# Attention and FFN on one core: another order of weight words, low parts, tanh product and attention in the first sixteen FFN steps

## The chip, the cores and the metric

The kernel runs on one core of a Trainium2 chip. The metric is the device time of the whole program in microseconds, over several runs. PE is TensorE (matrix products), PEld its weight loads, DVE is VectorE, ACT is ScalarE, POOL is GpSimd and SP is the engine whose queue issues the transfers.

## The reference

```python
# attention: batch 8, heads 8, sequence 576, head_dim 64
scores = scale * np.matmul(q, k.transpose(0, 1, 3, 2))
mask_local = (rel >= 0) & (rel < 32)                          # heads 0 to 3
mask_strided = (rel >= 0) & (pos[None, :] % 32 == pos[:, None] % 32)   # heads 4 to 7
scores = np.where(masks, scores, -1e9); scores -= max
attn = exp(scores) / (sum(exp(scores)) + 1e-9)
x = (attn @ v) as (4608 tokens, 512)
# FFN: w_in 512 x 2048, w_out 2048 x 512
h = x @ w_in
g = h * (1 / (1 + exp(-1.702 * h)))
out = g @ w_out
```

All inputs and the output are float32.

## The kernel before

Matrix products of the FFN are made from high and low parts. A float32 operand is cast to fp32r (the high part) and the remainder is the low part; one product of two operands is three matmuls (high·high, high·low, low·high). In the tile names `gh`, `gl` are the parts of g, `xhl`, `xll` those of the local half of x, `xhs`, `xls` those of its strided half, and `w` holds both parts of a weight tile.

**FFN.** The 4608 tokens are 9 groups of 512, and the 2048 hidden columns 16 tiles of 128, so there are 144 steps (group, tile). In step s PE computes h of that step (`ffn1`, 12 matmuls of 512 columns) and, two steps late (`LAG`), the product of g with w_out, summed in four PSUM banks `o` over the 16 steps of a group (`ffn2`, 12 matmuls). `act` makes g from h: tanh on ACT, then `(tanh + 1) * h` on DVE into the tile `g`, then gh on ACT and gl on DVE. There are two buffers of gh and gl and one of `g`. Eight PSUM banks: two for scores (`s`), six for h, the value products `a` and the four `o`; a bank of h is free when DVE has read it for g.

**Weight words.** The weights come in a 64-bit form, two 32-bit halves for each element, and are put together on the core once, in group 0. There are 32 words (`items`), two for each step: word 2f-2 is tile f of w_in, word 2f-1 is tile f-2 of w_out, for f from 2 on. A word takes a load into `raw` (SP), a shift of one half (`shift`) and a scaling with sign of the other (`sign`, both on ACT, but every fourth shift on DVE), the join of both (`join`, DVE: the row `raw<-raw` by SCALAR_TENSOR_TENSOR), the cast to the high part (`high`, ACT: `w<-raw`) and the subtraction that gives the low part (`low`, DVE: `w<-raw,w`). `raw` tiles and `w` tiles come out of one pool of 32 slots, so a later tile takes the slot of an earlier one when the last reader of that is done. The load of word k+8 is issued behind `low(k)`. The last word has a tile of its own, `words`.

**Attention.** 42 pairs, strided (three for each batch) and local. A pair's stages are: scores on PE; masked scores and maxima on DVE (two SCALAR_TENSOR_TENSOR into `pr`, then TENSOR_REDUCE); eight exponentials on ACT with their sums; sum and reciprocal on DVE (`rinv`); scaling of `pr` on POOL; transpositions on DVE into `pt` (6 for a strided pair, 8 for a local one, 32x256 each); value products on PE into a bank `a`; and the two parts of x on ACT and DVE. Pairs 0 to 4 are done ahead of step 2 in a prologue, in which the transposing is done by PE (`turn_pr`, bank `t`) and scores go into the banks `s` and `u`. Pairs 5 to 10 (strided, local, strided, local, strided, strided) are spread over the steps of group 0, later ones over the following groups: `TURNS` names the step of the transpositions for each, scores stand two steps behind the transpositions of the pair before the last one, the value products two steps behind a pair's own transpositions.

**What sets the order.** Each engine runs its instructions in the order in which the program writes them; `InOrder` (line 116, and 118 in the changed kernel) records every instruction, so that all rows have that one line and the tile names tell them apart. The main loop starts at step 2. A step of before writes: h of step s; then `act(s - 1, weigh)`, that is tanh and product of the step before with one `weigh` (high, shift and sign of the next, low, join of the next) between product and gh; a second `weigh`; transpositions, values; then scores, maxima and exponentials; then `ffn2(s - 2)`.

Of the kernel before, what the change touches and what calls it, by code (L numbers as in the profile page):

```python
# [9 lines left out]
F32 = mybir.dt.float32  # L10
# [8 lines left out]
P = 128  # L19
# [6 lines left out]
KB = QB + STRIDE  # L26
# [14 lines left out]
G = 512  # L41
NG = B * S // G
NF = DFF // P
# [12 lines left out]
AHEAD = 2  # L56
# [1 line left out]
RAWB = 8  # L58
N0 = 5
ZEROS = {0: 4, 1: 4}  # L60
TURNS = ((4, 7, 9, 12, 13), (0, 3, 6, 9, 12), (2, 8))


def _pairs():
# [17 lines left out]
def attn_ffn(ctx, tc, lqk, sqk, lv, sv, w_in, w_out, masks, out):  # L82
# [7 lines left out]
    ffn = ctx.enter_context(tc.tile_pool(name="ffn", bufs=2))  # L90
    psum = ctx.enter_context(tc.tile_pool(name="psum", bufs=8, space=bass.MemoryType.PSUM))

    def bank(name):
        tag, n = ("s", 2) if name[0] == "s" else ("x", 6)
        return psum.tile([P, 512], F32, tag=tag, name=name, bufs=n)

    def st2(shape, dtype, name):
        return st.tile(shape, dtype, tag="st2", name=name, bufs=NT)
# [5 lines left out]
    n0 = N0  # L104

    class InOrder:
# [15 lines left out]
    vector, scalar, gpsimd, sync, tensor = (  # L122
        InOrder(e) for e in (nc.vector, nc.scalar, nc.gpsimd, nc.sync, nc.tensor)
    )
    matmul, transposed = tensor.matmul, tensor.transpose
# [3 lines left out]
    def w_tile(shape, dtype, name):  # L129
        return wp.tile(shape, dtype, tag="w", name=name, bufs=2 * NF)  # L130
# [32 lines left out]
    zeros = const.tile([P, P], BF16, name="zeros")  # L163
# [3 lines left out]
    first = [[bank(f"{x}{j}") for j in range(2)] for x in "sut"]  # L167
# [8 lines left out]
    def geom(p):  # L176

        kind, a, _ = pairs[p]
        if kind == "s":
            m = masks_sb[:, :NB]  # L180
            return NB, m.unsqueeze(1).broadcast_to([P, 2 * U, NB])
        begins = [i for i in range(2 * U) if (2 * U * a + i) % (S // QB) == 0]
        if not begins:
            m = masks_sb[:, MASK_L + KB : MASK_L + 2 * KB]
            return KB, m.unsqueeze(1).broadcast_to([P, 2 * U, KB])
        at = MASK_L + (0, 2, 3, 1)[begins[0]] * KB
        m = masks_sb[:, at : at + U * KB]
        return KB, m.unsqueeze(1).broadcast_to([P, 2, U * KB])
# [107 lines left out]
    def turn_pr(p):  # L296

        nk, _ = geom(p)
        for i in range(HU):
            n = i % (2 * U)  # L300
            transposed(
                first[2][i // (2 * U)][:nk, n * P : (n + 1) * P], prs[p % AHEAD][:, i, :nk], ident_sb
            )
# [85 lines left out]
    items = [(0, 0), (1, 0)]  # L389
# [3 lines left out]
    raws, words, highs = {}, {}, {}  # L393

    def load_w(k):

        f, m = items[k]
        raws[k] = w_tile([P, DM, 2], U32, f"raw_{k}")
        sync.dma_start(out=raws[k], in_=(w_in, w_out)[m][f])

    def shift(k, engine):

        l = raws[k][:, :, 0]
        if engine is scalar:
            scalar.activation(
                l, raws[k].bitcast(U8)[:, :, 3], AF.Copy, scale=1 / 32, bias=-15.5 / 32  # L410
            )
        else:
            vector.tensor_scalar(
                out=l, in0=l, scalar1=29, scalar2=None, op0=ALU.logical_shift_right
            )

    def sign(k):
        h = raws[k][:, :, 1]
        words[k] = h if k < len(items) - 1 else st2([P, DM], U32, "words")
        scalar.activation(  # L420
            words[k].bitcast(F32), h.bitcast(F32), AF.Prelu, scale=2.0**-112, alpha=2.0**32
        )

    def join(k):
        vector.scalar_tensor_tensor(
            out=words[k], in0=words[k], scalar=3, in1=raws[k][:, :, 0],
            op0=ALU.logical_shift_left, op1=ALU.bitwise_or,
        )

    def high(k):  # L430
        f, m = items[k]
        part = w_tile([P, 2, DM], F32R, f"w_{f}_{m}")
        hi, lo = highs[k] = [part[:, i] for i in range(2)]
        if m:
            woh[f], wol[f] = hi, lo
        else:
            wih[f], wil[f] = (x.rearrange("p (c n) -> p c n", c=NC) for x in (hi, lo))
        scalar.copy(out=hi, in_=words[k].bitcast(F32))

    def low(k):  # L440
        hi, lo = highs.pop(k)
        vector.tensor_tensor(
            out=lo, in0=words.pop(k).bitcast(F32), in1=hi.bitcast(F32), op=ALU.subtract
        )
        if k + RAWB < len(items) - 1:
            load_w(k + RAWB)
        elif k == len(items) - 2:
            load_w(k + 1)

    made = [0]  # L450

    def weigh():

        k = made[0]
        made[0] += 1
        if k < len(items):
            high(k)
        if k + 1 < len(items) and k + 1 in raws:
            if (k + 1) % 4:
                shift(k + 1, scalar)  # L460
            sign(k + 1)
        if k < len(items):
            low(k)
            if k + 1 < len(items):
                if (k + 1) not in words:
                    shift(k + 1, scalar)
                    sign(k + 1)
                elif not (k + 1) % 4:
                    shift(k + 1, vector)
                join(k + 1)  # L470

    hps, gs, outs = {}, {}, {}

# [11 lines left out]
                    stop=closes and c == cs[-1] and m == 2,  # L485
                )

    def act(s, beside=lambda: None):
        ps = hps.pop(s)
        g2 = ffn.tile([P, G], F32, tag="g2", name=f"g2_{s}", bufs=1)  # L490
        scalar.activation(g2, ps, AF.Tanh, scale=0.851)
        vector.scalar_tensor_tensor(
            out=g2, in0=g2, scalar=1.0, in1=ps, op0=ALU.add, op1=ALU.mult
        )
        beside()
        gh, gl = gs[s] = [
            ffn.tile([P, G], F32R, tag=f"g{x}", name=f"g{x}_{s}", bufs=LAG) for x in "hl"
        ]
        scalar.copy(out=gh, in_=g2)
        vector.tensor_tensor(out=gl, in0=g2, in1=gh.bitcast(F32), op=ALU.subtract)  # L500
# [24 lines left out]
    def run(gen, n=HU):  # L525
        for _ in range(n):
            next(gen, None)


    steps = [(j, f) for j in range(NG) for f in range(NF)]  # L530
# [30 lines left out]
    def scaled(p):  # L561
        run(halfway.pop(p))

    def late_part(p):
        run(valued.pop(p))

    def value_products(p):
        valued[p] = values(p)
        run(valued[p], 1)

    for i in range(n0):
        if i + 1 < n0:
            scores(i + 1)
            nothing(ZEROS.get(i, 0))
        if i >= 1:
            run(halfway[i - 1], 1)
        if i >= 3:
            late_part(i - 3)
        if i >= 1:
            scaled(i - 1)  # L580
        if i >= 2:
            fetch_pt(i - 2)
        if i + 1 < n0:
            maxima(i + 1)
        else:
            shift(0, vector)
            sign(0)
        halfway[i] = softmax(i)
        run(halfway[i], 2)
        if i >= 2:  # L590
            fetch_pt(i - 2, 1)
        run(halfway[i], 2)
        if i >= 2:
            value_products(i - 2)
            run(valued[i - 2], 1)
        if i >= 1:
            turn_pr(i - 1)

    late_part(n0 - 3)
    run(halfway[n0 - 1], 1)  # L600
    scaled(n0 - 1)
    fetch_pt(n0 - 2)
    fetch_pt(n0 - 2, 1)
    join(0)
    value_products(n0 - 2)
    weigh()
    run(valued[n0 - 2], 1)
    turn_pr(n0 - 1)
    ffn1(0, (2, 3), closes=False)
# [1 line left out]
    fetch_pt(n0 - 1)  # L611
    fetch_pt(n0 - 1, 1)
    value_products(n0 - 1)
    weigh()
    run(valued[n0 - 1], 1)
    ffn1(1, (2, 3), closes=False)
    late_part(n0 - 1)
    ffn1(0, (0, 1), opens=False)
    weigh()
    ffn1(1, (0, 1), opens=False)  # L620
    for p in (n0, n0 + 1):
        load_qk(p)
        load_v(p)
    act(0, weigh)

    turn = {}
    p = n0
    for j, w in enumerate(windows):
        for i in range(len(w)):
            turn[p] = j * NF + TURNS[0 if j == 0 else 1 if len(w) > 2 else 2][i]  # L630
            p += 1
    begin = {p: max(2, turn.get(p - AHEAD, 0) + 2) for p in turn}
    turning, soft = {}, {}
    for s in range(2, len(steps) + LAG):
        if s < len(steps):
            ffn1(s)
        if s <= len(steps):
            act(s - 1, weigh)
        weigh()
        for p, t in turn.items():  # L640
            if t == s:
                turning[p] = transpose(p)
            if t <= s <= t + 1:
                run(turning[p], 2)
            if t + 2 == s:
                parts = values(p)
                run(parts)
                load_v(p + 2)
        for p, t in turn.items():
            if begin[p] == s:  # L650
                scores(p)
                load_qk(p + AHEAD)
                maxima(p)
                soft[p] = softmax(p)
            elif begin[p] < s < t:
                run(soft[p], -(-(s - begin[p]) * 4 // (t - 1 - begin[p])) - -(-(s - 1 - begin[p]) * 4 // (t - 1 - begin[p])))
                if s == t - 1:
                    run(soft.pop(p))
        if s >= LAG:
            ffn2(s - LAG)  # L660

# [91 lines left out]
```

## Time and profile before

| | us |
|---|---|
| median of three runs (lowest, highest) | 920.68 (920.41, 921.74) |
| the profiled execution | 919.76 |
| its span | 918.0 |
| PE busy | 898.0 (98%) |
| DVE busy | 462.1 (50%) |
| ACT busy | 368.6 (40%) |
| POOL busy | 54.2 (6%) |
| start of h of step 16, the first without weight words | 141.90 |

Times in rows are microseconds from the start of the span; the profiled execution's time holds about 1.8 us outside the span. A row of the timeline shows start, duration, engine, operation, written tile and read tiles, and in brackets the idle time before it with what ended it. A row of the waits shows total, count and longest.

### The profile page before, as it was taken

What the parts mean: (1) busy time and instruction counts of PE and PEld (TensorE: products, weight loads), DVE (VectorE), ACT (ScalarE), POOL (GpSimd) and SP (SyncE); (2) the same over time, 40 slices, a digit from 0 to 9 for tenths busy, and PEclk for the clock granted to TensorE, in tenths of its full rate; (3) what the DMA queues carried; (4) which work ended last, traced back from release to release, by engine and by line L of the source; (5) the groups of instructions that cost most, each with busy time, mean ns of one, the idle gap of its engine ahead of it and who ended that gap; (6) DMA issues with size and microseconds to landing.
All of it is one profiled execution on the core that took longest, in us unless ns stands there. A gap on an engine that the chain in (4) does not pass through costs nothing.

```text
span 918.0 us, 14635 instructions
## 1 busy us (share of the span) xinstructions
PE 898.0 (98%) x5834; PEld 722.1 (79%) x5834; DVE 462.1 (50%) x893; ACT 368.6 (40%) x1122; POOL 54.2 (6%) x60
## 2 busy tenths in 40 slices
PE   8799889999999999999999999999999999999998
PEld 5687667888888888888887888888888888888886
DVE  4778886544455545454644545544455344223222
ACT  7678756432433333333433344333443332222221
POOL 4001001000000000010000000000010000000000
PEclk9799999999999999999999999999999999999999
DMA  9854413111211112121211221111220010001001
GB/s 308 297 209 173 142 56 121 38 39 33 74 62 62 33 44 78 39 71 44 78 38 38 65 78 49 38 33 58 67 79 18 19 46 1 1 1 46 0 1 47
DMA packets 21813, 62.43 MB, mean 68 GB/s; under 512 B 2608, under 2 KB 2992, under 8 KB 21744
## 3 DMA queue, kind: packets, MB, share of 16 engines
q1 hardware_dynamic: 21744, 61.49, 19.9%
q8 instruction: 46, 0.75, 0.3%
q14 instruction: 23, 0.19, 0.1%
HBM read 52.04 MB, written 9.44 MB: 67 GB/s over the span
## 4 chain that ended last, share of the span: by engine, by line
PE 87%; DVE 6%; ACT 5%; issue 1%; DMA 0%; DVEq 0%; ACTq 0%
PE o L116 41%; PE h L116 39%; PE a L116 4%; PE s L116 3%; DVE raw L116 2%; ACT raw L116 1%; ACT pr L116 1%; ACT w L116 1%; PE t L116 1%; DVE w L116 1%; DVE pt_l L116 1%; DVE pt_s L116 1%; DVE g L116 1%; DMA raw<-w_out 0%; DVE pr L116 0%
## 5 line engine op out<-in xcount | busy, mean ns | idle before, releaser
L116 PE MATMUL o<-w,gh 128*128 128x512 f32 x1152 | 367.2, 400 | 0.0
L116 PEld LDWEIGHTS o<-w,gh 128*128 128x128 f32 x1152 | 214.4, 189 | 51.8 <-issue 0.2
L116 PE MATMUL o<-w,gl 128*128 128x512 f32 x576 | 228.5, 397 | 0.0
L116 PE MATMUL h<-xhl,w 128*128 128x512 f32 x576 | 201.5, 391 | 0.6 <-DVE xls L116 0.5
L116 PE MATMUL h<-xhs,w 128*128 128x512 f32 x576 | 202.0, 391 | 0.0
L116 ACT CAST gh<-g 128x512 fp32r<-128x512 f32 x144 | 89.2, 620 | 265.0 <-PE o L116 184.7
L116 DVE TENSOR_TENSOR gl<-g,gh 128x512 fp32r<-128x512 f32 x144 | 99.5, 691 | 169.2 <-ACT gh L116 169.2
L116 DVE SCALAR_TENSOR_TENSOR g<-g,h 128x512 f32<-128x512 f32 x144 | 98.5, 684 | 130.1 <-ACT g L116 128.9
L116 ACT ACTIVATE g<-h 128x512 f32<-128x512 f32 x144 | 85.3, 592 | 132.2 <-PE h L116 128.9
L116 PEld LDWEIGHTS o<-w,gl 128*128 128x128 f32 x576 | 108.7, 189 | 26.1
L116 PEld LDWEIGHTS h<-xhl,w 128*128 128x128 f32 x576 | 108.0, 188 | 25.9 <-DVE xls L116 1.5
L116 PEld LDWEIGHTS h<-xhs,w 128*128 128x128 f32 x576 | 108.3, 188 | 22.7
L116 PE MATMUL h<-xll,w 128*128 128x512 f32 x288 | 112.3, 390 | 0.0
L116 PE MATMUL h<-xls,w 128*128 128x512 f32 x288 | 112.1, 389 | 0.0
L116 ACT ACTIVATE pr<-pr,nmax 128x96 f32<-128x96 f32 (+1 forms) x296 | 101.8, 346 | 0.0
L116 POOL TENSOR_TENSOR pr<-pr,rinv 128x432 f32<-128x432 f32 (+1 forms) x42 | 48.4, 1152 | 707.4 <-ACT g L116 478.2
L116 PEld LDWEIGHTS h<-xll,w 128*128 128x128 f32 x288 | 54.1, 188 | 12.2
L116 PEld LDWEIGHTS h<-xls,w 128*128 128x128 f32 x288 | 54.2, 188 | 11.3
L116 DVE STREAM_TRANSPOSE pt_l<-pr 32x256 f32<-32x256 f32 x128 | 55.6, 434 | 1.5
L116 ACT ACTIVATION_READ_ACCUMULATOR pr<-pr,nmax 128x1 f32 x296 | 55.8, 188 | 0.0
L116 DVE STREAM_TRANSPOSE pt_s<-pr 32x256 f32<-32x256 f32 x126 | 54.8, 435 | 1.4
L116 PE MATMUL s<-qk 64*64 64x54 f32 (+1 forms) x1280 | 32.9, 242 | 5.0 <-DVE pr L116 5.0
(56 smaller groups left out, 428.5 us busy)
## 6 DMA issues: line engine op xcount, KB each, us to landing
qk<-sqk SPq DMA_DIRECT2D x23, 452.0 KB, 4.2
qk<-lqk SPq DMA_DIRECT2D x18, 576.0 KB, 4.9
out<-out SPq DMA_DIRECT2D x36, 256.0 KB, 2.1
raw<-w_in SPq DMA_DIRECT2D x16, 512.0 KB, 10.0
raw<-w_out SPq DMA_DIRECT2D x16, 512.0 KB, 9.8
v<-lv SPq DMA_DIRECT2D x18, 384.0 KB, 3.9
v<-sv SPq DMA_DIRECT2D x24, 256.0 KB, 2.8
qk<-sqk SPq DMA_DIRECT2D x2, 226.0 KB, 2.8
```

Source lines behind the costliest of these rows:

```text
L116: ins = call(*args, **kw)
```

## The change

The prologue gets six products of a 128x128 tile of zeros (`IDLE`) behind `turn_pr(1)` and `turn_pr(2)`, written into columns of the bank `u` or `s` that scores don't use. In the main loop the parts of a step stand in another order. On DVE: sum and reciprocal of the pair whose transpositions come in this step, both joins, gl of the step before, both lows, the product g of this same step, then transpositions, low part of x, maxima. On ACT: gh of the step before, both highs, shift and sign of word 2s+2, tanh of this step, shift and sign of word 2s+3, exponentials, high part of x. All shifts but the first stand on ACT. `TURNS` of group 0 and the rule for `begin` (the step of the scores) move with it: scores(5) stand in step 2 and scores(6) in step 4, which were both in step 2.

```diff
-TURNS = ((4, 7, 9, 12, 13), (0, 3, 6, 9, 12), (2, 8))
+IDLE = 6
+IDLE_AT = 4 * KB
+TURNS = ((5, 7, 9, 11, 13), (0, 3, 6, 9, 12), (2, 8))
...
-    def weigh():
-
-        k = made[0]
-        made[0] += 1
-        if k < len(items):
-            high(k)
-        if k + 1 < len(items) and k + 1 in raws:
-            if (k + 1) % 4:
-                shift(k + 1, scalar)
-            sign(k + 1)
-        if k < len(items):
-            low(k)
-            if k + 1 < len(items):
-                if (k + 1) not in words:
-                    shift(k + 1, scalar)
-                    sign(k + 1)
-                elif not (k + 1) % 4:
-                    shift(k + 1, vector)
-                join(k + 1)
+    def begin_word(k, engine=scalar):
+
+        if k < len(items):
+            if k not in raws:
+                load_w(k)
+            shift(k, engine)
+            sign(k)
...
+    def weigh(k):
+
+        high(k)
+        begin_word(k + 1)
+        low(k)
+        join_word(k + 1)
...
-    def act(s, beside=lambda: None):
+    def act(s):
         ps = hps.pop(s)
...
-        beside()
+
+    def split(s):
+        g2 = g2s.pop(s)
         gh, gl = gs[s] = [
...
+        if 2 <= i < n0 - 1:
+            for _ in range(IDLE):
+                matmul(first[(i + 1) % 2][0][:, IDLE_AT:], lhsT=zeros, rhs=zeros, start=True, stop=True)
...
-    act(0, weigh)
+    act(0)
+    weigh(3)
+    split(0)
+    begin_word(5)
+    act(1)
...
-    begin = {p: max(2, turn.get(p - AHEAD, 0) + 2) for p in turn}
+    begin = {p: turn[p - AHEAD] + 2 if p - AHEAD in turn else turn[p] - 3 for p in turn}
...
-        if s <= len(steps):
-            act(s - 1, weigh)
-        weigh()
+        last = len(items) - 1
+        now = [k for k in (2 * s, 2 * s + 1) if k < last] + [last] * (s == NF)
         for p, t in turn.items():
+            if t == s:
+                run(soft.pop(p))
+        if now == [last]:
+            begin_word(last)
+            split(s - 1)
+        for k in now:
+            join_word(k)
+        if now != [last] and s <= len(steps):
+            split(s - 1)
+        for k in now:
+            high(k)
+        for k in now[:1]:
+            if k + 2 < last:
+                begin_word(k + 2)
+        for k in now:
+            low(k)
+        if s < len(steps):
+            act(s)
+        if len(now) == 2 and now[1] + 2 < last:
+            begin_word(now[1] + 2)
+        if s == NF - 1:
+            load_w(last)
...
```

Three places in the order of the instructions follow; numbers in names tell buffers apart.

DVE before, from the reciprocal of pair 7 in step 8 to the masked scores of pair 8 (`g_8` is the product of step 8, made in step 9; `raw<-raw` are joins, or a shift where it is TENSOR_SCALAR; `w` are lows):

```order
L116 TENSOR_SCALAR rinv_1002<-ssum_945 128x8
L116 RECIPROCAL rinv_1002<-rinv_1002 128x8
L116 SCALAR_TENSOR_TENSOR g_8_1031<-g_8_1031,h_962 128x512
L116 TENSOR_TENSOR w_0_1034<-raw_781,w_0_1034 128x512
L116 SCALAR_TENSOR_TENSOR raw_792<-raw_792 128x512
L116 TENSOR_TENSOR gl_1043<-g_8_1031,gh_1042 128x512
L116 TENSOR_TENSOR w_1_1046<-raw_792,w_1_1046 128x512
L116 TENSOR_SCALAR raw_831<-raw_831 128x512
L116 SCALAR_TENSOR_TENSOR raw_831<-raw_831 128x512
L116 TENSOR_TENSOR xll<-a_1054,xhl 128x2x256
L116 STREAM_TRANSPOSE pt_s<-pr_95 32x8x32 x6
L116 SCALAR_TENSOR_TENSOR pr_94<-s_8_1081,masks_sb 128x384
```

DVE in the changed kernel, from the product of step 8 to the masked scores of pair 8 in step 9:

```order
L118 SCALAR_TENSOR_TENSOR g_8_1004<-g_8_1004,h_973 128x512
L118 TENSOR_SCALAR rinv_1043<-ssum_1009 128x8
L118 RECIPROCAL rinv_1043<-rinv_1043 128x8
L118 SCALAR_TENSOR_TENSOR raw_791<-raw_791 128x512
L118 SCALAR_TENSOR_TENSOR raw_794<-raw_794 128x512
L118 TENSOR_TENSOR gl_1050<-g_8_1004,gh_1049 128x512
L118 TENSOR_TENSOR w_0_1053<-raw_791,w_0_1053 128x512
L118 TENSOR_TENSOR w_1_1055<-raw_794,w_1_1055 128x512
L118 SCALAR_TENSOR_TENSOR g_9_1065<-g_9_1065,h_1030 128x512
L118 STREAM_TRANSPOSE pt_s<-pr_95 32x8x32 x6
L118 TENSOR_TENSOR xll<-a_1076,xhl 128x2x256
L118 SCALAR_TENSOR_TENSOR pr_94<-s_8_1097,masks_sb 128x384
```

The reciprocal of pair 7 now has both joins of step 9 right behind it, the lows stand behind both joins and gl, the step's own product behind the lows, and the shift is gone.

ACT before, where the eight exponentials of pair 7 stand (CAST `w` are highs, `raw` x2 is shift and sign of a word):

```order
L116 ACTIVATE pr_95,ssum_945<-pr_95,nmax_885 128x54 x4
L116 ACTIVATE g_7_975<-h_901 128x512
L116 CAST w_0_978<-raw_725 128x512
L116 ACTIVATE raw_737<-raw_737 128x512 x2
L116 CAST gh_986<-g_7_975 128x512
L116 CAST w_1_990<-raw_737 128x512
L116 ACTIVATE raw_781<-raw_781 128x512 x2
L116 ACTIVATE pr_95,ssum_945<-pr_95,nmax_885 128x54 x4
L116 ACTIVATE g_8_1031<-h_962 128x512
```

ACT in the changed kernel, step 8 with the eight exponentials of pair 7, and the head of step 9:

```order
L118 CAST gh_988<-g_7_911 128x512
L118 CAST w_0_992<-raw_711 128x512
L118 CAST w_1_994<-raw_714 128x512
L118 ACTIVATE raw_791<-raw_791 128x512 x2
L118 ACTIVATE g_8_1004<-h_973 128x512
L118 ACTIVATE raw_794<-raw_794 128x512 x2
L118 ACTIVATE pr_95,ssum_1009<-pr_95,nmax_957 128x54 x8
L118 CAST gh_1049<-g_8_1004 128x512
L118 CAST w_0_1053<-raw_791 128x512
```

The exponentials stood in two fours, one in each of two steps; now all eight stand at the end of one step, behind both words' shifts and the step's tanh.

PE in the changed kernel, at the second place with zeros in the prologue, behind the products that turn pair 2 (`t`):

```order
L118 MATMUL a_93<-pt_s,v_152 64x2x54 x8
L118 MATMUL t_90<-ident_sb,pr_94 54x128 x4
L118 MATMUL t_91<-ident_sb,pr_94 54x128 x4
L118 LDWEIGHTS zeros
L118 MATMUL s_86<-zeros 128x128
```

Between the products `t_91` and the values `a_92`, which were neighbours, stand six products of zeros, each with its weight load (the first is shown); `s_86` is the bank that the next exponentials of the prologue read.

More of the change, by code (lines that the diff above doesn't have):

```diff
@@ L446, in low, with join_word @@
             load_w(k + RAWB)
-        elif k == len(items) - 2:
-            load_w(k + 1)
-    made = [0]
-    def weigh():
-        k = made[0]
-        made[0] += 1
-        if k < len(items):
-            high(k)
-        if k + 1 < len(items) and k + 1 in raws:
-            if (k + 1) % 4:
-                shift(k + 1, scalar)
-            sign(k + 1)
-        if k < len(items):
-            low(k)
-            if k + 1 < len(items):
-                if (k + 1) not in words:
-                    shift(k + 1, scalar)
-                    sign(k + 1)
-                elif not (k + 1) % 4:
-                    shift(k + 1, vector)
-                join(k + 1)
+    joined = set()
+    def begin_word(k, engine=scalar):
+        if k < len(items):
+            if k not in raws:
+                load_w(k)
+            shift(k, engine)
+            sign(k)
+    def join_word(k):
+        if k < len(items) and k not in joined:
+            joined.add(k)
+            join(k)
+    def weigh(k):
[3 more added lines that the diff above has]
+        join_word(k + 1)
     hps, gs, outs = {}, {}, {}
@@ L486, in ffn1 @@
                 )
-    def act(s, beside=lambda: None):
+    g2s = {}
+    def act(s):
         ps = hps.pop(s)
-        g2 = ffn.tile([P, G], F32, tag="g2", name=f"g2_{s}", bufs=1)
+        g2 = g2s[s] = ffn.tile([P, G], F32, tag="g2", name=f"g2_{s}", bufs=1)
         scalar.activation(g2, ps, AF.Tanh, scale=0.851)
@@ L585, in attn_ffn @@
         else:
-            shift(0, vector)
-            sign(0)
+            begin_word(0, vector)
         halfway[i] = softmax(i)
@@ L603, in attn_ffn @@
     fetch_pt(n0 - 2, 1)
-    join(0)
+    join_word(0)
     value_products(n0 - 2)
-    weigh()
+    weigh(0)
     run(valued[n0 - 2], 1)
@@ L613, in attn_ffn @@
     value_products(n0 - 1)
-    weigh()
+    weigh(1)
     run(valued[n0 - 1], 1)
@@ L618, in attn_ffn @@
     ffn1(0, (0, 1), opens=False)
-    weigh()
+    weigh(2)
     ffn1(1, (0, 1), opens=False)
@@ L636, in attn_ffn @@
             ffn1(s)
-        if s <= len(steps):
-            act(s - 1, weigh)
-        weigh()
+        last = len(items) - 1
+        now = [k for k in (2 * s, 2 * s + 1) if k < last] + [last] * (s == NF)
         for p, t in turn.items():
+            if t == s:
[20 more added lines that the diff above has]
+            load_w(last)
+        for p, t in turn.items():
+            if begin[p] < s < t:
+                n = t - 1 - begin[p]
+                i = s - begin[p]
+                run(soft[p], 4 * i // n - 4 * (i - 1) // n)
             if t == s:
@@ L644, in attn_ffn @@
                 run(turning[p], 2)
+        for p, t in turn.items():
             if t + 2 == s:
-                parts = values(p)
-                run(parts)
+                run(values(p))
                 load_v(p + 2)
-        for p, t in turn.items():
+        for p in turn:
             if begin[p] == s:
@@ L654, in attn_ffn @@
                 soft[p] = softmax(p)
[L655 to L658, printed above, removed]
         if s >= LAG:
```

## The prediction

> **What bounds the kernel now.** I read the page's busy shares first, then busy time by stretches, then the waits of the first 150 us, then the chain that ended last.
>
> ```profile
> span 918.0 us, 14635 instructions
> core 0: us, PE busy (x) PEld busy (x) DVE busy (x) ACT busy (x) POOL busy (x), PEclk, DMA share, GB/s
> 40.00:45.00 5.00, 0.97 (x18) 0.96 (x22) 3.95 (x8) 4.46 (x9) 0.00 (x0) 0.78 0.41 142
> 45.00:50.00 5.00, 5.00 (x33) 3.92 (x26) 3.77 (x6) 0.50 (x1) 0.00 (x0) 0.54 0.62 204
> 125.00:130.00 5.00, 2.22 (x52) 2.11 (x56) 4.78 (x10) 2.86 (x6) 0.00 (x0) 0.81 0.01 2
> 150.00:918.00 768.00, 764.12 (x4759) 618.35 (x4757) 351.30 (x680) 262.23 (x799) 36.15 (x31) 1.00 0.14 45
> ```
>
> From 150 us on PE is busy 764.12 of 768.00 us at full clock, and the change leaves PE's work there as it is. So the end moves by as much as the start of step 16, the first step without weight words, moves. Ahead of it PE stands idle in places, and behind the longer gaps its clock is low (0.54 in 45 to 50). In 125 to 130 DVE is busy 4.78 of 5 us and PE 2.22: there DVE sets the pace.
>
> ```profile
> PE a L116 <- DVE g L116: 7.3, 3, 3.9
> PE s L116 <- DVE pr L116: 5.0, 1, 5.0
> DVE rinv L116 <- ACT pr L116: 3.7, 3, 1.8
> ```
>
> ```profile
> 133.85 0.39 PE L116 MATMUL h<-xhl,w 128*128 128x512 f32 x1
> ...
> 141.90 0.49 PE L116 MATMUL h<-xhl,w 128*128 128x512 f32 x1 [0.45 <-DVE xls L116]
> ```
>
> ```profile
> 34.42 0.61 ACT g L116
> ...
> 86.73 1.29 ACT pr L116 x8
> ...
> 102.34 1.43 ACT pr L116 x8
> ...
> 141.90 3.04 PE h L116 x12
> ```
>
> The change goes for the first two waits: scores(6) waits 5.0 us for maxima(5), and value products wait 7.3 us in three places for a product's bank. The chain gives the two ends of my sum: the first tanh at 34.42 and step 16 at 141.90. Between them it runs nearly all on ACT and DVE, so I follow those two queues, each in its own order, and let PE follow. Prices per instruction (start to next start):
>
> ```profile
> 103.67 0.58 ACT L116 ACTIVATE g<-h 128x512 f32<-128x512 f32 x1
> 104.14 0.65 ACT L116 CAST w<-raw 128x512 fp32r<-128x512 f32 x1
> 104.68 1.26 ACT L116 ACTIVATE raw<-raw 128x512 uint32<-128x512 uint8 x2
> 105.83 0.62 ACT L116 CAST gh<-g 128x512 fp32r<-128x512 f32 x1
> 106.70 0.67 ACT L116 CAST w<-raw 128x512 fp32r<-128x512 f32 x1 [0.25 <-DVE raw L116]
> ```
>
> ```profile
> 88.06 0.17 DVE L116 TENSOR_SCALAR rinv<-ssum 128x8 f32<-128x8 f32 x1 [0.60 <-ACT pr L116]
> 88.54 0.69 DVE L116 SCALAR_TENSOR_TENSOR g<-g,h 128x512 f32<-128x512 f32 x1
> 89.14 0.95 DVE L116 TENSOR_TENSOR w<-raw,w 128x512 fp32r<-128x512 f32 x1
> ...
> 94.01 2.67 DVE L116 STREAM_TRANSPOSE pt_s<-pr 32x256 f32<-32x256 f32 x6
> 96.71 1.02 DVE L116 SCALAR_TENSOR_TENSOR pr<-s,masks_sb 128x384 f32<-128x384 f32 x2
> ...
> 98.64 0.68 DVE L116 SCALAR_TENSOR_TENSOR g<-g,h 128x512 f32<-128x512 f32 x1
> ...
> 104.28 0.69 DVE L116 SCALAR_TENSOR_TENSOR g<-g,h 128x512 f32<-128x512 f32 x1 [1.21 <-ACT g L116]
> ...
> 105.97 0.69 DVE L116 SCALAR_TENSOR_TENSOR raw<-raw 128x512 uint32<-128x512 uint32 x1 [0.40 <-ACT raw L116]
> 106.58 0.68 DVE L116 TENSOR_TENSOR gl<-g,gh 128x512 fp32r<-128x512 f32 x1
> ...
> 132.01 0.66 DVE L116 SCALAR_TENSOR_TENSOR pr<-s,masks_sb 128x216 f32<-128x216 f32 x2
> ...
> 133.23 0.68 DVE L116 SCALAR_TENSOR_TENSOR g<-g,h 128x512 f32<-128x512 f32 x1
> ```
>
> ACT: tanh 0.47, high 0.55, shift with sign 1.13 (1.15 in these rows, a little less elsewhere), four exponentials 1.29 (strided) or 1.43 (local). DVE: 0.61 for a 128x512 operation; sum and reciprocal 0.48 to the next; a transposition 0.45, so six (strided) 2.70 and eight (local) 3.57; maxima 1.93 (96.71 to 98.64, local) or 1.22 (132.01 to 133.23, strided). Handed over: join to high 0.73 (105.97 to 106.70), tanh to product 0.61 (103.67 to 104.28).
>
> **The change, part by part.** *The front, steps 2 to 7.* From tanh(0) ACT now does tanh, high, shift with sign, gh, shift with sign, tanh(1), and by the prices tanh(2) starts at 42.3, maxima(5) at 43.5, and step 3's first join at 44.7. No scores wait for another pair's maxima any more, so the 5.0 us and the low clock behind them go. With four exponentials in each of steps 3 and 4, step 5's first join follows at 56.9, step 6's, behind six transpositions, at 63.8, step 7's at 70.5.
>
> *The rounds of two steps, 7 to 14.* Counted from the first join of an even step: second high 0.60 + 0.73 = 1.33, shift with sign from 1.88, tanh 3.01, shift with sign from 3.48, exponentials from 4.62. All eight stand there, 2.58 or 2.86, and the odd step's sum and reciprocal stand ahead of its joins on DVE, so these wait for the last: 4.62 + 2.58 + 0.13 (86.73 + 1.29 to 88.06, and 0.09 by which the last one outlasts its pitch) + 0.48 = 7.81 (strided), 8.09 (local). DVE stands idle about 3 us meanwhile. In the odd step tanh starts at 3.01, product 3.62, transpositions 4.23; these, then the low part of x (0.5 to 0.6) and the next pair's maxima fill DVE up to the even step's first join: 9.52 (8 transpositions, strided maxima), 9.46 (6, local), 9.52, 8.75 (6, strided). From step 7 to step 14 that is 9.52 + 7.81 + 9.46 + 8.09 + 9.52 + 7.81 + 8.75 = 61.0, and step 14's first join comes at 131.5. Here the serial order costs what the front won: exponentials no longer run beside DVE's work, and transpositions and maxima no longer beside ACT's. That the seven shifts leave DVE (0.42 each) is in this count, and so is the one more ACT operation for each word.
>
> *To step 16.* h of step 15 needs low(28), 1.81 to 2.50 after that join, at its third matmul, so it starts 2.05 behind the join. From h of step 15 to that of step 16 PE did the same work before in 141.90 - 0.45 - 133.85 = 7.60. Step 16: 131.5 + 2.05 + 7.60 = 141.15, which is 0.75 before 141.90; step 16 itself, not held by xls, may save 0.25 of its 3.04. So far -1.0.
>
> *A wait that is added.* The pool `w` has 32 slots. With both highs ahead of the lows, high(25), high(27) and high(29) of steps 12, 13 and 14 take the slots of words 24, 26 and 28, which are free only when low(24), low(26), low(28) have read them. Such a low is the fourth operation on DVE, 1.81 to 2.50 behind the first join: high starts at 2.55 instead of 1.33, and with it all behind it on ACT, shift with sign, tanh, exponentials, and DVE's product and transpositions. No row of before has this wait: at least 0, if ACT is late anyway, at most 3 x 1.22 = 3.7. The third delays only what PE reaches later. I take two: +2.4.
>
> *POOL beside the joins.* POOL's scaling of pr now starts 0.25 behind the reciprocal, in the first join.
>
> ```profile
> 23.85 1.47 POOL L116 TENSOR_TENSOR pr<-pr,rinv 128x768 f32<-128x768 f32 x1 [0.86 <-DVE rinv L116]
> 88.64 0.91 POOL L116 TENSOR_TENSOR pr<-pr,rinv 128x432 f32<-128x432 f32 x1 [13.04 <-ACT g L116]
> ...
> 24.77 1.10 DVE L116 SCALAR_TENSOR_TENSOR raw<-raw 128x512 uint32<-128x512 uint32 x1
> ```
>
> In these rows a join and a low (89.14) that began while POOL scaled ended only after it did, 1.10 and 0.95 for 0.69. By them the second join (start 0.60, free end 1.29) ends at about 1.7 for strided and 2.3 for local pairs: 0.41 in steps 5, 9, 13 and 0.97 in steps 7, 11, together 3.2, on the path each time. Bounds: 0, if POOL waits instead, and 5.4, if already the first join is held. The Trainium skill, "SBUF — State Buffer", section "Who interferes with whom", says "Issue order, not op shape, decides who blocks", the first of the two holding the ports for its whole instruction; the trace agrees where POOL came first (88.64 ahead of 89.14). The case that DVE comes first is the second rival below. I take 3.2, since back-to-back joins leave a moment between them in which POOL, waiting, may come first as it did at 88.64.
>
> *The zero products.* Six 128-column products behind turn_pr(1) and turn_pr(2) write into the bank that the next exponentials read, and these now wait for them.
>
> ```profile
> 18.75:22.35 3.60, 1.77 (x21) 1.15 (x19) 2.48 (x5) 3.55 (x19) 1.54 (x2) 0.99 1.02 350
> 22.35:25.70 3.35, 3.00 (x24) 2.33 (x25) 2.64 (x5) 0.68 (x4) 1.70 (x2) 0.50 1.02 410
> ```
>
> ```profile
> 5.30 2.26 PE t L116 x10
> ...
> 24.91 1.97 PE a L116 x30
> ...
> 30.36 1.08 PE a L116 x32
> ```
>
> A 512-column one takes 0.226, so six of a quarter take at least 0.34, and at most 1.36 if they cost as much. ACT is busy 3.55 of 3.60 us there, so a delay stays: about 0.9 at the first place and 0.6 at the second, +1.5 (0 to 3.0). Against it, PE is fuller in 18.75 to 22.35 (now 1.77 of 3.60), and the half clock of 22.35 to 25.70 may not come: the value products would take 1.08 instead of 1.97. But DVE's copy ahead of the next ones (30.36) is no earlier, so about 0.5 of it reaches tanh(0). Net +1.0, between -0.6 and +3.0.
>
> *The clock.* PE will wait 3 to 5 us ahead of h in steps 9, 11, 13 and 15, since the even step's joins come late. After 3.9 us (the longest of the 7.3) the clock was 0.81 in 125 to 130, after 5.0 it was 0.54. Only the last of these gaps is without slack behind it: +0.9, between 0 and 1.7 (half of a 3.4 us stretch).
>
> SP's queue has the same loads; words are asked for behind each low as before and land steps ahead, and the last word is begun a step later than it is now, with PE's product for it another step off. I cost that at nothing; if the load came 3 us late, step 17 would pay it.
>
> Sum: -1.0 + 2.4 + 3.2 + 1.0 + 0.9 = +6.5. The profiled execution took 919.76, so 926.3; that execution is 0.92 under the median of the runs, 920.68, and I leave the number there, a little to the low side.
>
> **The rivals.** *The reciprocal's wait stays short (faster).* Place: the head of steps 7, 9, 11, 13. Before, DVE waited 3.7 us in three places for exponentials, 0.60 at 88.06. Were it 0.6 again instead of 1.8, 3.0, 3.3 and 3.0, the rounds would shrink by 8.7: 926.3 - 8.7 = 917.6. It decides once more than 6.5 of the 8.7 goes. For it: ACT has idle time in every odd step. Against it: the order has all eight exponentials behind two shifts with sign and the tanh.
>
> *POOL waits for DVE.* Joins and lows hold POOL off, it scales behind the lows, from 3.1 to 4.0 or 4.6, and delays transpositions by at most 0.4 in two steps: 926.3 - 3.2 + 0.4 = 923.5. For it: the first join begins before POOL does. Against it: the frozen rows above.
>
> *All bounds dear.* Zero products 3.0, POOL ahead of the first join 5.4, clock 1.7: 926.3 + 2.0 + 2.2 + 0.8 = 931.3; one or two of them, 928 to 930.
>
> *The added costs vanish.* No slot wait, no freezing, no zero delay, no clock loss: 919.76 - 1.0 = 918.8, up to 922 with one of them.
>
> **How the numbers follow.** Forecast 0.42 (its own range 924 to 928.5), POOL waits 0.24, dear 0.12, costs vanish 0.12, short reciprocal wait 0.10. No change means within 0.2% of 920.68, 918.84 to 922.52, about what a measurement of this kernel can tell. Slower: forecast, dear and six tenths of POOL waits, 0.69. Faster: the short wait and a little of the vanished costs, 0.12. The rest, 0.19, is the same. The range 920.3 to 930.5 leaves out the short wait and some of both ends.
>
> **What would show it.** Right: no wait of scores for maxima near 40; DVE waiting about 3 us for exponentials at the reciprocal of steps 9, 11, 13; high of 25, 27 and 29 released by a low 1.2 us late; second joins of 1.1 to 1.7 us beside POOL; step 7's first join near 71 to 72, step 14's near 138, h of step 16 near 148. Wrong: a round of two steps under 16.3, joins of 0.69 beside POOL, or step 16 before 142.

## Result: 0.9% slower, and the profile after

| | before | changed |
|---|---|---|
| median, us | 920.62 (920.41 to 921.74) | 929.32 (928.45 to 929.77) |
| ratio, 95% interval | | 1.0091 (1.0073 to 1.0108) |
| profiled execution; its span | 919.76; 918.0 | 929.77; 928.0 |
| first tanh, us from the start | 34.42 | 37.58 |
| h of step 16 | 141.90 | 152.04 |

Busy time of the changed kernel in stretches (same columns as before):

```profile
span 928.0 us, 14672 instructions
45.00:50.00 5.00, 5.00 (x23) 4.05 (x23) 4.12 (x9) 4.05 (x9) 0.00 (x0) 1.00 1.01 395
115.00:120.00 5.00, 3.61 (x9) 2.83 (x10) 4.28 (x11) 2.58 (x6) 0.00 (x0) 0.50 0.78 270
130.00:135.00 5.00, 1.85 (x8) 1.14 (x7) 4.15 (x7) 2.60 (x5) 1.16 (x1) 0.99 0.33 115
135.00:140.00 5.00, 3.43 (x8) 2.76 (x9) 4.08 (x9) 2.88 (x6) 0.00 (x0) 0.50 0.02 3
160.00:928.00 768.00, 764.14 (x4759) 618.46 (x4757) 365.00 (x678) 261.02 (x802) 38.46 (x31) 1.00 0.14 45
```

From step 16 on nothing changed: PE is busy 764.14 of 768.00 us, as it was, and the end moved by 10.0 as h of step 16 moved by 10.1. The early stall is gone (45 to 50: PE busy 5.00 at full clock, 0.54 before). The loss is in the later rounds, where PE waits more than before and then runs at half clock (0.50 in 115 to 120 and 135 to 140).

Waits of the first 150 us of the changed kernel (total, count, longest):

```profile
ACT w L118 <- DVE raw L118: 29.8, 17, 4.7
PE h L118 <- DVE g L118: 13.9, 4, 4.7
DVE rinv L118 <- ACT pr L118: 11.1, 4, 3.3
ACT w L118 <- DVE w L118: 4.0, 3, 1.8
```

The two waits that the change went for (PE for maxima 5.0, value products 7.3) are not among the large ones any more. In their place stand h products that wait for a product g (13.9 in four places), reciprocals that wait for exponentials (11.1, it was 3.7), highs that wait for a join (29.8, it was 9.8, since the joins stand behind these reciprocals), and highs that wait for a low, which before did not exist.

One round of DVE, steps 8 and 9, and the head of step 11:

```profile
85.00 1.29 DVE L118 SCALAR_TENSOR_TENSOR raw<-raw 128x512 uint32<-128x512 uint32 x2
...
88.66 0.69 DVE L118 SCALAR_TENSOR_TENSOR g<-g,h 128x512 f32<-128x512 f32 x1 [0.56 <-ACT g L118]
92.33 0.17 DVE L118 TENSOR_SCALAR rinv<-ssum 128x8 f32<-128x8 f32 x1 [2.99 <-ACT pr L118]
...
92.66 1.96 DVE L118 SCALAR_TENSOR_TENSOR raw<-raw 128x512 uint32<-128x512 uint32 x2
...
102.81 1.28 DVE L118 SCALAR_TENSOR_TENSOR raw<-raw 128x512 uint32<-128x512 uint32 x2
...
110.73 2.52 DVE L118 SCALAR_TENSOR_TENSOR raw<-raw 128x512 uint32<-128x512 uint32 x2
```

```profile
92.91 1.16 POOL L118 TENSOR_TENSOR pr<-pr,rinv 128x432 f32<-128x432 f32 x1 [16.75 <-ACT gh L118]
110.98 1.72 POOL L118 TENSOR_TENSOR pr<-pr,rinv 128x768 f32<-128x768 f32 x1 [16.91 <-ACT gh L118]
```

DVE is idle for 2.99 us ahead of the reciprocal, and both joins stand behind it. The two joins take 1.28 where POOL is quiet (102.81), 1.96 beside the strided scaling and 2.52 beside the local one. The round from 85.00 to 102.81 is 17.8.

The highs of words 25, 27 and 29 on ACT, and the end of the chain on PE:

```profile
124.05 0.65 ACT L118 CAST w<-raw 128x512 fp32r<-128x512 f32 x1 [1.08 <-DVE w L118]
...
133.56 0.65 ACT L118 CAST w<-raw 128x512 fp32r<-128x512 f32 x1 [1.82 <-DVE w L118]
...
143.48 0.65 ACT L118 CAST w<-raw 128x512 fp32r<-128x512 f32 x1 [1.06 <-DVE w L118]
```

```profile
135.82 0.70 DVE g L118
...
136.57 5.38 PE h L118 x12
141.95 2.80 PE o L118 x12
144.75 2.74 PE h L118 x12
```

The chain of step 14 goes from the product of step 13 to h of step 14, which takes 5.38 instead of 2.74: it starts behind a wait of 4.7 and runs at half clock (0.50 in 135 to 140).

### The profile page after: what moved, and what is told of

It reads as the page before. It is cut to its first block, busy times and chain, and to the rows that moved or that the text cites. A ratio compares the mean times of both kernels' runs of the same rounds, so it can differ in the third digit from the quotient of the medians.

```text
span 928.0 us, 14672 instructions
## 1 busy us (share of the span) xinstructions
PE 902.9 (97%) x5846; PEld 723.4 (78%) x5846; DVE 477.0 (51%) x886; ACT 370.9 (40%) x1129; POOL 58.1 (6%) x60
## 4 chain that ended last, share of the span: by engine, by line
PE 86%; ACT 6%; DVE 5%; issue 1%; DMA 0%; SPq 0%; ACTq 0%; DVEq 0%
PE o L118 40%; PE h L118 39%; PE a L118 4%; PE s L118 3%; ACT raw L118 2%; ACT pr L118 2%; DVE raw L118 2%; ACT w L118 1%; DVE pt_l L118 1%; ACT g L118 1%; PE t L118 1%; DVE g L118 1%; DVE pt_s L118 0%; DVE pr L118 0%; DMA qk<-sqk 0%
## 5 line engine op out<-in xcount | busy, mean ns | idle before, releaser
L118 PE MATMUL h<-xhl,w 128*128 128x512 f32 x576 | 205.7, 399 | 14.8 <-DVE g L118 13.9
L118 PE MATMUL h<-xhs,w 128*128 128x512 f32 x576 | 204.9, 397 | 0.0
L118 DVE TENSOR_TENSOR gl<-g,gh 128x512 fp32r<-128x512 f32 x144 | 112.7, 783 | 135.1 <-ACT gh L118 134.0
L118 PEld LDWEIGHTS h<-xhl,w 128*128 128x128 f32 x576 | 109.9, 191 | 42.7 <-DVE g L118 15.7
L118 PEld LDWEIGHTS h<-xhs,w 128*128 128x128 f32 x576 | 110.3, 192 | 24.0 <-DVE w L118 0.4
L118 POOL TENSOR_TENSOR pr<-pr,rinv 128x432 f32<-128x432 f32 (+1 forms) x42 | 52.3, 1245 | 715.3 <-DVE rinv L118 634.3
L118 PEld LDWEIGHTS h<-xll,w 128*128 128x128 f32 x288 | 55.1, 191 | 12.4
L118 ACT ACTIVATE raw<-raw 128x512 f32<-128x512 f32 (+1 forms) x62 | 38.2, 668 | 2.0 <-DMA raw<-w_out 2.0
```

Of the source, the lines that this page charges most:

```text
L118: ins = call(*args, **kw)
```

## Experiments

Times are medians against the kernel before on the same chip (920.08 to 920.76 there). Differences named "less" are against 929.32. Since the first tanh also moves between executions (below), the stretch from it to h of step 16 is given beside the median; it is 107.5 before and 114.5 in the changed kernel.

**1. No zeros.**

```diff
-IDLE = 6
+IDLE = 0
```

> The changed kernel with IDLE = 0: no products of zeros in the prologue. Theory (the zeros delay the exponentials of the prologue, and the half clock that was on weaker ground at 22 to 29 us now falls on the products of h ahead of the first tanh): the first tanh goes back from 37.58 to about 34.4, where it was before, and all that follows with it: 3.2 less, about 926.1. Rival (the zeros pay for themselves, the first tanh is late for another reason, such as POOL slowed by a join): at most 0.5 less, 928.8 or more. Half way (the delay goes, the half clock stays): 1.2 to 2 less, 927.5.

926.64, ratio to before 1.0064 (1.0050 to 1.0078): 2.7 less. First tanh at 34.98; from there 113.6 to h of step 16. The first theory holds by its total. What its half clock costs is not so plain: see experiment 5. The 0.9 less behind the first tanh is not in the waits of the rounds, which are the same (13.9 of PE for g, 11.1 of the reciprocals): h of step 8 takes 3.05 instead of 4.61 and h of step 14 4.52 instead of 5.38. Where PE's half clock falls moves from one execution to another, so a difference under 1 us in this stretch can't be put down to an edit.

**2. No scaling on POOL for pairs 5 to 9.**

```diff
         vector.reciprocal(out=rinv, in_=rinv)
+        if n0 <= p < n0 + 5:
+            return
         gpsimd.tensor_tensor(
```

> The changed kernel without POOL's scaling of pr for pairs 5 to 9 (their attention stays unnormalised; this is left out). Theory (both joins behind the reciprocal are held while POOL scales, 0.66 us too long for a strided and 1.23 for a local pair, on the path in steps 5, 7, 9, 11, 13): joins of 0.69 there, and 3 x 0.66 + 2 x 1.23 = 4.4 less, about 924.9. Rival (the joins' delay is slack, since tanh waits for ACT or PE in those steps): under 1 less. The low clock of PE behind each gap stays in both.

924.17, 1.0035 (1.0023 to 1.0047): 5.2 less. From the first tanh (36.17) it is 110.1 to h of step 16, 4.4 less than in the changed kernel, which is near the joins' held time of 4.5; the rest is the earlier first tanh. As far as the movement of the clock in experiment 1 lets one tell, the delay is on the path in full.

**3. A slot for high(25) and high(27).**

```diff
-        if k + RAWB < len(items) - 1:
+        if k + RAWB < len(items) - 2:
             load_w(k + RAWB)
+        elif k == 26:
+            load_w(30)
```

> The changed kernel with the load of word 30 issued behind low(26) instead of low(22), so that the pool of 32 slots has a free one for high(25) and high(27) in steps 12 and 13; high(29) still waits for low(28). Theory (these two waits of 1.2 us each are on the path): ACT's wait for a low goes from three times to once, the products of steps 12 and 13 come 1.2 earlier each, 2.4 less, about 926.9. Rival (in these steps PE's wait for the bank or its half clock ends last, so that the wait is slack): 0 to 0.5 less. If word 30 came too late, step 14 would wait for its load and it would be slower.

927.29, 1.0061 (1.0046 to 1.0076): 2.0 less, and 111.5 from the first tanh (38.26), 3.0 less. The wait of two highs on the 32 slots is on the path; with it some of PE's low clock goes (h of step 14 takes 4.61 instead of 5.38).

**4. Joins ahead of the reciprocal.**

```diff
-        for p, t in turn.items():
-            if t == s:
-                run(soft.pop(p))
...
         for k in now:
             join_word(k)
+        for p, t in turn.items():
+            if t == s:
+                run(soft.pop(p))
```

> The changed kernel with both joins of a step ahead of the sum and reciprocal of the pair that is turned in it, instead of behind them. Theory (the joins of steps 7, 9, 11, 13 wait about 3 us for the last exponentials, and with them the highs, the tanh and the transpositions): joins no longer wait for exponentials, highs start right behind gh, transpositions come 1.1 to 1.5 earlier in each of four rounds, 4 to 6 less, 923 to 925. Rival A (ACT is the bound: the highs stand behind the exponentials on ACT anyway, and POOL now holds gl and the lows instead of the joins, so that all is given back): within 1 of 929. Rival B (PE's bank wait ends last): 0 to 2 less.

921.61, 1.0006 (0.9997 to 1.0015): 7.7 less, and no longer to be told from before. Not all of it is the edit's: the first tanh stands at 36.01 instead of 37.58, ahead of anything that the edit touches. From there it is 108.3 to h of step 16, 6.2 less, at the upper end of the theory (4 to 6). DVE in steps 8 and 9 of this kernel:

```profile
81.29 1.28 DVE L118 SCALAR_TENSOR_TENSOR raw<-raw 128x512 uint32<-128x512 uint32 x2
...
85.53 1.29 DVE L118 SCALAR_TENSOR_TENSOR raw<-raw 128x512 uint32<-128x512 uint32 x2
88.62 0.17 DVE L118 TENSOR_SCALAR rinv<-ssum 128x8 f32<-128x8 f32 x1 [1.80 <-ACT pr L118]
...
89.74 2.00 DVE L118 TENSOR_TENSOR w<-raw,w 128x512 fp32r<-128x512 f32 x2
91.85 0.69 DVE L118 SCALAR_TENSOR_TENSOR g<-g,h 128x512 f32<-128x512 f32 x1
...
97.69 1.28 DVE L118 SCALAR_TENSOR_TENSOR raw<-raw 128x512 uint32<-128x512 uint32 x2
```

The joins run under the exponentials. POOL now holds the two lows (2.00 for 1.28), which end while tanh is still running, and the round is 16.4 (81.29 to 97.69) instead of 17.8. Rival A, that POOL's hold gives all back on the lows, falls. PE's waits for g fall from 13.9 to 8.4 as well; how much of the 6.2 came by way of them and the half clock behind was not measured apart.

**5. The zeros alone, in the kernel before.** The six products behind `turn_pr(1)` and `turn_pr(2)`, as in the change, and nothing else.

> The kernel before with nothing but the six products of zeros behind turn_pr(1) and turn_pr(2) added. Theory (the zeros cost what the prologue's exponentials wait for them, plus a half clock that moves to the products ahead of the first tanh): first tanh from 34.42 to about 37, and 2.7 more at the end, about 923.4. Rival (they pay in the kernel before, since its half clock of 22 to 29 us goes and its queues are others): 0.5 less to 0.5 more.

922.36, 1.0015 (1.0003 to 1.0026): 1.8 more than before, between the two expectations. The prologue's stretch ahead of the first tanh in three profiles, the changed kernel, this one, and the kernel of experiment 8, which has no zeros:

```profile
32.50:36.00 3.50, 3.50 (x24) 2.88 (x21) 2.03 (x4) 2.30 (x4) 0.00 (x0) 0.52 1.08 362
```

```profile
32.50:36.00 3.50, 3.50 (x23) 2.86 (x18) 2.22 (x4) 2.56 (x5) 0.00 (x0) 1.00 1.07 349
```

```profile
32.50:36.00 3.50, 3.50 (x17) 2.87 (x16) 2.28 (x4) 2.84 (x6) 0.00 (x0) 1.00 1.06 349
```

Their first tanh stands at 37.58, 35.72 and 35.08. With the clock full in all of the prologue, the zeros cost 0.64 (35.72 against 35.08), or 0.93 by experiment 4 (36.01). A half clock in 32.5 to 36 costs about 1.6 more (37.58 against 36.01 in experiment 4, which has the same prologue and full clock there). It is not tied to the zeros: the kernels of experiments 6 and 7 have none and show 0.64 and 0.60 in that stretch. PE is busy only 2.05 to 2.22 of the 3.45 us before that stretch, in all of these; what decides whether the clock then falls stays open.

**6. The stall alone.** The kernel before, with pair 6 begun in step 4.

```diff
+    begin[n0 + 1] = 4
```

> The kernel before with scores(6), maxima(6) and its exponentials begun in step 4 instead of step 2, all else as it is. Theory (the removed stall is real gain and was paid back by the rounds in the changed kernel): PE's wait of 5.0 us for maxima goes, step 4 starts about 5 earlier, and since ACT and DVE have the same work afterwards, 3 to 5.5 less, about 916.5. Rival (DVE is the bound from step 5 on and only fills up earlier, or the load of the last word ends last): 0 to 1 less.

919.86, 0.9989 (0.9978 to 1.0000): 0.7 less, hardly clear of no change, and at the rival's end. By one execution of each, and counted from the first tanh, the fifth one comes at 20.8 instead of 26.4: 5.6 are won. The sixth comes at 30.7 instead of 32.9, the last of group 0 at 107.7 instead of 109.1: in step 5 3.3 are lost again, and at the end 1.4 are left. There PE has a new wait and ACT, too:

```profile
63.90 0.47 PE L116 MATMUL h<-xhl,w 128*128 128x512 f32 x1 [1.73 <-DVE g L116]
```

```profile
63.84 0.62 ACT L116 CAST gh<-g 128x512 fp32r<-128x512 f32 x1 [3.52 <-DVE g L116]
```

So 5.0 us of a stalled engine were worth about 1.4 at the end of the phase and 0.7 of the time.

**7. The three edits together** (1, 3 and 4).

> The changed kernel without zeros, with word 30 loaded later and with the joins ahead of the reciprocal: the three edits together. If they add up as they measured alone (2.7, 2.0 and 7.7 less): 916.9. If they share a part (the low clock behind the bank waits, which each of them shortens): 917 to 919. If only the joins count: 921.

917.72, 0.9967 (0.9957 to 0.9978): 11.6 less than changed, where the three alone sum to 12.4. From the first tanh (36.37) it is 104.7 to h of step 16, 9.7 less, where the three alone sum to about 10. Faster than before by 0.3%.

**8. Shift and sign behind the tanh.** Experiment 7 with all begins of words from step 2 on written out, each behind the step's tanh, and from step 5 on in the odd steps only (word 30 in step 14):

```diff
+BEGINS = {
+    2: (6, 7), 3: (8, 9), 4: (10, 11), 5: (12, 13, 14, 15), 7: (16, 17, 18, 19),
+    9: (20, 21, 22, 23), 11: (24, 25, 26, 27), 13: (28, 29), 14: (30,),
+}
...
-        for k in now[:1]:
-            if k + 2 < last:
-                begin_word(k + 2)
...
-        if len(now) == 2 and now[1] + 2 < last:
-            begin_word(now[1] + 2)
+        for k in BEGINS.get(s, ()):
+            begin_word(k)
```

> The kernel of the three edits together, with shift and sign of words taken out of ACT's queue ahead of the tanh: from step 5 on all four of two steps stand behind the tanh of the odd step, where ACT waits 4.5 us for DVE's transpositions and maxima. Theory (ACT's row from the even step's first high through the exponentials to the odd step's tanh sets the round): that row gets 3 x 1.13 shorter, rounds of about 16.4 shrink to 13 to 13.5, where PE's own 12.8 is next, 8 to 10 less than the three edits alone, 907 to 910. Rival (the odd step's end gets ACT late, or loads of words come late, or DVE with 13 us of work in a round is next): 0 to 4 less.

908.14, 0.9860 (0.9845 to 0.9876): 9.6 less than experiment 7, the theory's end, and faster than both kernels. From the first tanh (35.08) it is 95.5 to h of step 16, 9.3 less. ACT and DVE in steps 8 and 9:

```profile
79.72 0.60 ACT L122 ACTIVATE g<-h 128x512 f32<-128x512 f32 x1
80.22 0.33 ACT L122 ACTIVATE pr<-pr,nmax 128x54 f32<-128x54 f32 x1
...
84.48 0.60 ACT L122 ACTIVATE g<-h 128x512 f32<-128x512 f32 x1
84.97 4.58 ACT L122 ACTIVATE raw<-raw 128x512 uint32<-128x512 uint8 x8
89.38 0.63 ACT L122 CAST xhl<-a 128x512 fp32r<-128x512 f32 x1
```

```profile
77.74 1.29 DVE L122 SCALAR_TENSOR_TENSOR raw<-raw 128x512 uint32<-128x512 uint32 x2
...
90.04 0.69 DVE L122 TENSOR_TENSOR xll<-a,xhl 128x512 fp32r<-128x512 f32 x1 [0.78 <-ACT xhl L122]
...
92.56 1.28 DVE L122 SCALAR_TENSOR_TENSOR raw<-raw 128x512 uint32<-128x512 uint32 x2
```

The two tanh of a round stand 4.8 apart, and four words (4.58) fill time in which ACT waited: its wait for the next join is 2.98 and 2.75 now, 5.03 and 4.49 in experiment 4. The round is 14.8, not 13 to 13.5: xhl now stands behind these words and holds xll and the maxima up by 0.78, POOL still holds the lows by 0.72, and the reciprocal still waits 0.31. PE's waits for g are down to 0.2 and its clock over the span is 0.999.

**9. Experiment 8 with zeros.**

> The fastest kernel so far (shift and sign moved, 908.1) with the products of zeros back in the prologue. Theory (the zeros' own price is the delay of the prologue's exponentials; first tanh 35.72 and 36.01 in runs with them, 35.08 without, all three at full clock): 0.6 to 0.9 more, about 909. Rival (they also bring a half clock ahead of the first tanh each time, as in the changed kernel's profile, 37.58): 2.5 to 3 more, about 911. Rival (no price, since PE's work in the rounds takes the lead up): 908.

909.60, 0.9880 (0.9861 to 0.9898): 1.5 more than experiment 8. First tanh 36.59, with 0.65 of the clock in 29 to 32.5: between the theories, like experiment 5. Behind the first tanh nothing differs (95.4 and 95.5 to h of step 16).

**10. Experiment 8 with the reciprocal ahead of the joins.**

> The fastest kernel so far with the sum and reciprocal back ahead of the joins, as in the changed kernel. Theory (the joins then wait for the last exponential, about 5.2 behind the even step's first join, and for POOL, 0.66 or 1.23): high and tanh of steps 7, 9, 11 and 13 come 1.5 to 2.1 later, 6 to 8 more, 914 to 916. Rival (ACT's highs stand behind the exponentials in any case, and the joins are no later than these): under 2 more.

914.03, 0.9926 (0.9904 to 0.9948): 5.9 more. The first tanh is the same (35.01 and 35.08), so that the order of joins and reciprocal alone is worth about as much here as in experiment 4 (101.3 against 95.5 behind the first tanh, 6.2 there), though the exponentials end about 2.1 earlier; it is just under the theory's lower end. DVE at the head of step 9 shows both of its causes, the wait for exponentials and the join held by POOL:

```profile
85.22 0.17 DVE L122 TENSOR_SCALAR rinv<-ssum 128x8 f32<-128x8 f32 x1 [1.50 <-ACT pr L122]
...
85.55 1.96 DVE L122 SCALAR_TENSOR_TENSOR raw<-raw 128x512 uint32<-128x512 uint32 x2
```

## Why the prediction was right, and where it was short

The direction and the mechanism held: the front wins, the rounds give back more than that. The forecast said 926.3, the profiled execution took 929.77 (median 929.32), inside the range, 3 above. That is outside the forecast's own 924 to 928.5, at the place that the prediction gave to "one or two" of the dear bounds, 928 to 930. Two terms were dear indeed: the zeros' place took 3.2, past its bound of 3.0, and POOL 4.5 of its 5.4. By the sum h of step 16 stands at 148.65 and by the trace at 152.04: 2.2 of the 3.4 is the zeros' term, 1.3 POOL's and 0.5 the way from step 14 to step 16, and the rest of the rounds and the front came 0.6 shorter than their sums.

**The rounds.** From join to join the prediction's round, with its own added waits, against the trace (85.00, 92.66 and so on): step 7 to 8 9.52 + 0.97 against 10.81, 8 to 9 7.81 against 7.66, 9 to 10 9.46 + 0.41 against 10.15, 10 to 11 8.09 against 7.92, 12 to 13 7.81 + 1.22 against 8.83. The reading of two in-order queues from start-to-start times was good to 0.2 us, and what differs more is POOL's share. The waits for exponentials, 1.86, 2.99, 3.28 and 3.01, stood where they were forecast (1.8, 3.0, 3.3, 3.0); the rival that they stay short is refuted, and experiments 4 and 10 show that they were on the path (6.2 and 5.8 from the first tanh to h of step 16).

**POOL beside the joins**, term 3.2: it was 4.5 (three times 0.68, twice 1.24), and experiment 2 shows it on the path (4.4). The step that failed is that POOL was taken to run from its start, 0.25 behind the first join's: its rows are 1.16 and 1.72 for 0.91 and 1.47, so it first waits for the first join, and the second join then waits for all of POOL. Both halves fit the rule of the Trainium skill, "SBUF — State Buffer", "Who interferes with whom", taken instruction by instruction. The times agree only roughly: POOL took 0.25 more, where the first join (92.66, 0.64) had 0.39 left. The rival that POOL waits for DVE's whole row of joins and lows fell: back-to-back issue did not keep POOL out, it came in behind one join.

**The slots**, term 2.4: the products of steps 12 and 13 stand 1.1 later each than those of other steps (126.33 is 4.80 behind its first join, 88.66 is 3.66 behind), and experiment 3 took back 2.0 of the median and 3.0 of the stretch behind the first tanh.

**The zeros**, term +1.0: the first tanh was 3.2 later. 0.6 to 0.9 of it is the zeros' own delay, near the term, and about 1.6 the half clock of 32.5 to 36, which the prediction did not have and which two kernels without zeros show, too (experiments 6 and 7). The last 0.7 is that the profiled execution of before (34.42) was early even among kernels without zeros (35.08 at full clock); why is not shown. By medians the zeros cost 2.7, 1.8 and 1.5 in three kernels. That a half clock of 22 to 29 would go and give back 0.5 was wrong: with a full clock there the first tanh was not earlier in any run.

**To step 16 and the clock**, terms 2.05 + 7.60 + 0.9: it was 11.1 from step 14's first join (140.96) to h of step 16, 0.5 more. The step that failed is where PE waits: the prediction let h of step 15 wait for low(28) and put PE's gaps ahead of the odd steps. In the trace they stand ahead of steps 8, 10, 12 and 14, for g of the odd step:

```profile
79.80 0.50 PE L118 MATMUL h<-xhl,w 128*128 128x512 f32 x1 [2.50 <-DVE g L118]
...
97.71 0.79 PE L118 MATMUL h<-xhl,w 128*128 128x512 f32 x1 [2.71 <-DVE g L118]
...
116.39 0.80 PE L118 MATMUL h<-xhl,w 128*128 128x512 f32 x1 [3.98 <-DVE g L118]
...
136.57 0.79 PE L118 MATMUL h<-xhl,w 128*128 128x512 f32 x1 [4.72 <-DVE g L118]
```

By the program's order of banks, the value product took one of the two free ones, so that the next h waits until g of the step before has been read. The bank wait that the change was to remove had moved from the value products to h, and grew from 7.3 to 13.9, with the half clock behind it. Only the last of the four lies on the chain that ended last, which runs over ACT and DVE up to the product at 135.82; what the other three cost was not tested alone. Behind the last one h of step 14 runs at half clock, and PE comes to h of step 15 at 144.59, 3.63 behind step 14's first join where the prediction had 2.05. The 1.6 between them stands where the prediction had 0.9 for the clock, within its bound of 1.7, and from there to h of step 16 it is 7.45 for 7.60. So the size of the loss was nearly right, and its place one step off.

**The front** came as forecast: step 3's first join 10.3 behind the first tanh in both, step 7's 36.6 against 36.1 + 0.4. Experiment 6 shows what that was worth in the order of before: a removed stall of 5.0 left 1.4 at step 16.

## What to carry to other kernels

A reduction or reciprocal at the head of a step makes everything behind it on its engine wait for another engine's last operation; put first what needs only old data (here the joins: about 6 us, in two kernels), and put work with slack into the row where an engine is known to wait (here shift and sign on ACT: 9.6 us). When parts are regrouped (all highs, then all lows), look at what the pool's slots and banks then wait for: the slot wait and the bank wait of h both came with the new order. A stall that is cut out of a phase bound by two other engines is worth what these can use, 1.4 of 5.0 us here. And give a difference between two kernels from a point behind the places where single executions differ: by medians alone the joins seemed to be worth 7.7.

## What was not expected of the hardware

The scaling on POOL and DVE's joins were served in turns: one join, then POOL to its end (1.16 or 1.72 with its wait), then the next join, so a back-to-back neighbour did not hold POOL off. And the first tanh moved between 34.4 and 36.9 us in kernels without zeros, and between 35.7 and 38.3 in those with them. The kernel before and that of experiment 6 are the same program up to the scores of step 2, behind the first tanh, and that stood at 34.42 with a half clock in 22 to 29 us and at 36.88 with 0.64 of the clock in 32.5 to 36. So a difference of 2 us in this part between two profiles need not come from a change.
